# Joined attention blocks: a wait through GpSimd in place of TensorE's drain between the halves of the own products

## The chip, the core and the metric

The kernel runs on one core of a Trainium2 chip. The core has four engines that compute: TensorE (PE; its weight loads are listed apart as PEld), VectorE (DVE), ScalarE (ACT) and GpSimd (POOL). SyncE (SP) issues the DMA transfers. Each engine works through its own queue in order, and engines wait for each other by semaphores. The metric is the time of one execution on the device in microseconds; lower is better.

## What is computed

A linear attention with a decaying state over 768 steps, for 4 batches of 8 heads with 48 features, and then a feed-forward layer with a leaky activation on its output:

```
for t in range(S):
    cur = u * k_t (outer) v_t
    y[:, :, t] = r_t @ (state + cur)
    state = w_t[:, None] * state + k_t (outer) v_t
x = y as [3072 tokens, 384]
h = x @ w_in                       # 384 -> 2048
g = max(h, 0) + alpha * min(h, 0)
out = g @ w_out                    # 2048 -> 384
```

## The kernel before

The attention is cut into 24 blocks, q = 0 to 23: 12 chunks of 64 steps, each for two pairs of batches. A block's loads are wd, kr, rk and nv (decays, keys and queries by feature, queries and keys by step, values). VectorE scales kr by products of decays; GpSimd multiplies rk (L407, two multiplications per block: by u, then by the keys) and VectorE sums it into cd (L410), from which ScalarE makes the diagonal of the block's weights `at` (L415). TensorE makes the scores (L439), which VectorE puts into `at` (L444). The state of each batch pair lives in St and is scaled by GpSimd (L425) and added to by VectorE (L589).

`outputs` emits a block's products on TensorE. All work in it is on quarters of the array, 64 rows by 64 columns. Its parts, in the order in which they are issued from block 8 on:

- `carried` (L509): queries times the old state, 16 products;
- the first half of the own products, `own(True)` (L490, recorded at L482): 8 products, `at` times the values nv, where the row half of the array agrees with the bank (`yb[0]` or `yb[1]`) that the product writes;
- the scores of the next block, `sc` (L435, recorded at L439), 16 products, when the next block is joined to this one;
- the new part of the state, `state` (L516, recorded at L524), 16 products, absent in the last chunk (blocks 22 and 23);
- `other` (L526): a drain of TensorE, and then the second half of the own products, `own(False)`, 8 products that write the same two banks from the other row half.

The two halves write the same banks from different row halves of the array, and the kernel is written so that they do not do this at the same time: the drain keeps them apart. The profile counts two weight loads for each of these products: 16 loads for 8 products, 32 for 16. Blocks 8 to 22 carry the scores of the following block with them: these fifteen are the joined blocks. In blocks 0 to 7 and in block 23 the drain follows the first half directly.

Between the blocks TensorE runs the feed-forward layer: `moe_up` (L677; a bank of nine products, then ScalarE's L683 and VectorE's L685 make pos, ScalarE's L690 and VectorE's L691 split it into gh and gl) and `moe_down` (L705). A check of the inputs runs beside it late in the kernel: SyncE loads raw tiles (L796) and ScalarE works on them (L804 and L813).

A planner written into the kernel sets the order of all engines' work beforehand, from durations that stand in the code. A whole block's products are one operation to it, so what stands inside an operation does not move the others. The order of each queue is then fixed.

Of the kernel before, what the change touches and what calls it, by code (L numbers as in the profile page):

```python
# [33 lines left out]
GT = 3 * P  # L34
ROWS = (slice(0, D), slice(64, R2))
FULL = (slice(0, 64), slice(64, P))
VW = H * 64


# [185 lines left out]
def fast_path(tc, wgt, flag, dmaj, nat, u, ud, vg, wts, alpha, out, part):  # L225
# [4 lines left out]
    nc = tc.nc  # L230
# [7 lines left out]
    with tc.tile_pool(name="const", bufs=1) as const, tc.tile_pool(name="psum", bufs=1, space=PSUM) as psum:  # L238
        def ring(name, shape, n, dtype=F32, pool=const, ordered=True):
            return Ring([pool.tile(shape, dtype, name=f"{name}_{i}") for i in range(n)], ordered)  # L240
# [4 lines left out]
        bank = ring("bank", [P, 512], 5, pool=psum, ordered=False)  # L245
# [24 lines left out]
        r_rk = ring("rk", [P, 2 * HD], 2)  # L270
        r_nv = ring("nv", [P, VW], 3)
        r_suf = ring("suf", [P, SC], 1)
# [12 lines left out]
        extra = Tensor(r_os), Tensor(r_pos)  # L285
# [16 lines left out]
        def c_mask():  # L302
            nc.gpsimd.memset(mask, 1)
            nc.gpsimd.affine_select(out=mask, in_=mask, compare_op=ALU.is_gt, fill=0,
                                    base=0, pattern=[[1, P]], channel_multiplier=-1)
            nc.gpsimd.tensor_copy(out=mask[FULL[1], 0:TK], in_=mask[FULL[1], TK:P])

        def c_ident2():
            for i in range(2):
                nc.gpsimd.tensor_copy(out=ident2[FULL[i]], in_=ident[FULL[i], i * TK:(i + 1) * TK])  # L310
        op("POOL", 0.4, c_ident2, r=["ident"], w=["ident2"])
# [36 lines left out]
        def load(q):  # L348
# [8 lines left out]
            if natural:  # L357
                op("SP", 0.4, lambda: nc.sync.dma_start(out=rk.ap, in_=nat[q, :, 0:2 * HD]), w=[rk], lat=1.1)
            op("SP", 0.4, lambda: nc.sync.dma_start(out=nv.ap, in_=nat[q, :, 2 * HD:2 * HD + VW]), w=[nv], lat=0.75)
            if q < GROUPS[0]:  # L360
# [69 lines left out]
        def scores(q):  # L430

            kr, nv, at = ready[q]
            sps = [Tensor(bank), Tensor(bank)]

            def products():  # L435
                for p in range(NP):
                    for o, i in ORDER:
                        ts = slice(i * TK, (i + 1) * TK)
                        nc.tensor.matmul(sps[o].ap[FULL[i], p * TK:(p + 1) * TK], lhsT=kr.ap[FULL[o], 0, p, ts],  # L439
                                         rhs=kr.ap[FULL[o], 1, p, ts], start=True, stop=True)  # L440

            def rest():
                for o in range(2):
                    op("DVE", 0.46, lambda o=o: nc.vector.copy_predicated(  # L444
                        out=at.ap[:, o], mask=mask[:, 0:TK].unsqueeze(1).broadcast_to([P, NP, TK]), data=pairs(sps[o].ap[:, 0:NP * TK], TK)),
                       r=["mask", sps[o]], w=[(at, o)])
            return products, [(kr, 0), (kr, 1)], sps, rest
# [15 lines left out]
        def outputs(q, nxt):  # L463
# [7 lines left out]
            kr, nv, at = ready.pop(q)  # L471
# [4 lines left out]
            yb = Tensor(r_op if g == 0 else bank), Tensor(bank)  # L476
            up = c < NC - 1
            open_, last = set(), [None]

            def mm(t, rows, cols, stop=False, **kw):  # L480

                last[0] = nc.tensor.matmul(t.ap[rows, cols], start=(t, rows.start) not in open_, stop=stop, skip_group_check=True, **kw)  # L482
                open_.add((t, rows.start))
                return last[0]

            def col(place, i):
                return slice(place % 2 * P + i * TK, place % 2 * P + (i + 1) * TK)


            def own(same):  # L490


                for j in range(2):
                    for o, e in ORDER:
                        i, p = o if same else 1 - o, 2 * j + e
                        h = o * NP + p
                        if g > 0 or 2 * o + j < KT:
                            mm(yb[o], FULL[e], col(j, i), not same, lhsT=nv.ap[FULL[i], h * 64:(h + 1) * 64],
                               rhs=at.ap[FULL[i], o, p, :])
                if g == 0:  # L500


                    for k in range(KT):
                        for e in range(2):
                            i = k // 2 if same else 1 - k // 2
                            mm(yb[k // 2], FULL[e], col(k, i), not same, lhsT=extra[q].ap[FULL[i], (2 * k + e) * 64:(2 * k + e + 1) * 64],
                               rhs=at.ap[FULL[i], 1, 2 + e, :])

            def carried():  # L509
                for j in range(2):  # L510
# [5 lines left out]
            def state(ub, u0, mm):  # L516
                for p in range(NP):
                    for i, o in ORDER:
                        h = o * NP + p
                        mm(ub[i], FULL[o], slice(u0 + p * D, u0 + (p + 1) * D), lhsT=kn[FULL[i], p, FULL[o]],  # L520
                           rhs=nv.ap[FULL[i], h * 64:h * 64 + D])
# [1 line left out]
            def alone(t, rows, cols, **kw):  # L523
                nc.tensor.matmul(t.ap[rows, cols], start=True, stop=True, **kw)  # L524

            def other():  # L526


                nc.tensor.drain()
                own(False)  # L530

            def take(last):

# [23 lines left out]
            if g == 0:  # L557
                def products():
                    own(True)
                    other()  # L560
                op("PE", 1.2, products, r=[(at, 0), (at, 1), nv, extra[q], "ident"], w=yb, kind="QQ", due=due_att[q] + 1.4)
                ub, u0 = (Tensor(bank), Tensor(bank)), 0
                op("PE", 0.5, lambda: state(ub, 0, alone), r=["kn", nv], w=ub, kind="QQ", due=due_att[q] + 10.0)
            else:
                sc, sc_r, sc_w, rest = scores(nxt) if nxt else (None, [], [], None)
                ub, u0 = (sc_w, 256) if nxt else (yb, 256)

                def products():
                    if up and not sc:
                        state(ub, u0, mm)  # L570
                    if c > 0:
                        carried()
                    own(True)
                    if sc:
                        sc()
                        if up:
                            state(ub, u0, alone)
                    other()
                t = 0.8 + (0.47 if c > 0 else 0) + (0.47 if up else 0) + (0.47 if sc else 0)
                op("PE", t, products, r=[(at, 0), (at, 1), nv, "kn", "ident", *([(f"St{m}", i) for i in range(2)] if c > 0 else []), (kr, 1), *sc_r],  # L580
                   w=[*yb, *sc_w], kind="QQ", due=due_att[q] + t)
# [265 lines left out]
def general_path(tc, wgt, dmaj, nat, u, wts, out, xd):  # L847
# [5 lines left out]
    with tc.tile_pool(name="g_st", bufs=1) as st, tc.tile_pool(name="g_wk", bufs=1) as wk, \  # L853
# [12 lines left out]
        for c in range(NC):  # L866
            with tc.For_i(0, TK, 1) as t:
# [10 lines left out]
                for b in range(B):  # L878
                    src = nv[c, b // 2][ds(t + b % 2 * TK, 1), 2 * HD:2 * HD + VW].rearrange("t (o p e) -> o (t p) e", o=2, e=64)[:, :, 0:D]
                    for o in range(2):  # L880
# [113 lines left out]
def layout(r, k, v, w, u, moe_w_in, moe_w_out, moe_alpha):  # L994
# [14 lines left out]
    def natural(a):  # L1009
        return a.reshape(NM, 2, H, NC, TK, D).transpose(3, 0, 1, 4, 2, 5).reshape(NQ, P, HD)  # L1010

    vp = np.zeros((NQ, P, H, 64), v.dtype)
    vp[..., :D] = natural(v).reshape(NQ, P, H, D)
    nat = np.concatenate([natural(r), natural(k), vp.reshape(NQ, P, VW)], axis=2)

# [42 lines left out]
```

## Time and profile before

| what | value |
|---|---|
| time, median of 3 runs | 527.22 us (526.35 to 529.82) |
| span of the profiled execution | 527.3 us |
| TensorE products busy | 506.4 us (96%) |
| TensorE weight loads busy | 475.4 us (90%) |
| VectorE busy | 346.3 us (66%) |
| ScalarE busy | 301.0 us (57%) |
| GpSimd busy | 74.5 us (14%) |

The page gives for the profiled execution its span alone; it stands 0.1 us above the median of the runs. Busy time of the products is not a measure of how well TensorE is used, since products overlap and their ends are modelled; idle times ahead of weight loads say more. In the views, "issue" means that an engine was idle and waited for nothing that the profile shows.

### The profile page before, as it was taken

How to read it: one execution, taken by the hardware profiler on the slowest of the kernel's cores; microseconds unless marked ns; L12 is line 12 of the kernel's file. 1: busy time of each engine (PE TensorE's matmuls, PEld its weight loads, DVE VectorE, ACT ScalarE, POOL GpSimd, SP SyncE). 2: the span in 40 equal slices, each digit the busy share in tenths (PEclk: the TensorE clock that was granted, in tenths of full speed). 3: DMA queues.
4: the chain of work that ended last, by engine and by line, in shares of the span. 5: the costliest groups of instructions: out<-in, count | busy, mean ns of one | idle time of the engine just before them, and what ended most of it. 6: DMA issues, size and time to landing. Idle time of an engine off the chain costs nothing.

```text
span 527.3 us, 13761 instructions
## 1 busy us (share of the span) xinstructions
PE 506.4 (96%) x5654; PEld 475.4 (90%) x5654; DVE 346.3 (66%) x657; ACT 301.0 (57%) x806; POOL 74.5 (14%) x100
## 2 busy tenths in 40 slices
PE   9996999999999999999999999999999999999993
PEld 8974677789999999999999989999999999999992
DVE  6989798999888988868336655577663434434331
ACT  4763754765344566656555556676776666633441
POOL 2011110352001534213000210121000000000000
PEclk9998999999999999999999999999999999999998
DMA  8877678765221668465423556346462035000101
GB/s 301 295 249 261 202 258 277 251 209 153 74 100 49 205 189 265 124 187 154 105 64 107 166 149 211 118 167 189 133 221 89 10 103 197 2 16 10 38 1 37
DMA packets 31945, 78.27 MB, mean 148 GB/s; under 512 B 4480, under 2 KB 13184, under 8 KB 31872
## 3 DMA queue, kind: packets, MB, share of 16 engines
q1 hardware_dynamic: 31872, 77.30, 46.5%
q8 instruction: 46, 0.75, 0.6%
q14 instruction: 27, 0.22, 0.1%
HBM read 66.27 MB, written 6.29 MB: 138 GB/s over the span
## 4 chain that ended last, share of the span: by engine, by line
PE 86%; DMA 6%; DVE 4%; issue 1%; ACT 1%; SPq 0%; DVEq 0%
PE bank L677 37%; PE op L705 33%; PE bank L482 6%; PE op L699 5%; DMA wl<-cx 3%; PE bank L439 2%; DMA raw<-in_wts_dram 2%; PE bank L457 1%; PE bank L524 1%; DMA kr<-in_dmaj_dram 1%; DVE suf L377 1%; PE bank L752 1%; DVE wd L383 0%; DVE cx L652 0%; DVE cx L648 0%
## 5 line engine op out<-in xcount | busy, mean ns | idle before, releaser
L677 PE MATMUL bank<-x,wh 128*128 128x384 f32 (+1 forms) x864 | 230.4, 328 | 0.4 <-ACT cd L403 0.3
L677 PEld LDWEIGHTS bank<-x,wh 128*128 128x128 f32 x864 | 153.5, 188 | 5.4 <-ACT at L415 0.7
L683 ACT ACTIVATE pos<-bank,alpha_n 128x384 f32<-128x384 f32 (+1 forms) x144 | 78.6, 546 | 110.5 <-PE bank L677 110.3
L677 PE MATMUL bank<-x,wl 128*128 128x384 f32 (+1 forms) x432 | 137.2, 318 | 0.0
L685 DVE SCALAR_TENSOR_TENSOR pos<-bank,pos 128x384 f32<-128x384 f32 (+1 forms) x144 | 73.5, 511 | 92.8 <-ACT pos L683 92.6
L705 PE MATMUL op<-wh,gh 128*128 128x384 f32 x336 | 112.9, 336 | 0.7 <-ACT gh L690 0.7
L705 PE MATMUL op<-wh,gl 128*128 128x384 f32 x336 | 112.5, 335 | 0.2 <-DVE gl L691 0.2
L705 PE MATMUL op<-wl,gh 128*128 128x384 f32 x336 | 112.5, 335 | 0.0
L691 DVE TENSOR_TENSOR gl<-pos,gh 128x384 fp32r<-128x384 f32 (+1 forms) x120 | 69.8, 582 | 50.3 <-ACT gh L690 49.3
L677 PEld LDWEIGHTS bank<-x,wl 128*128 128x128 f32 x432 | 81.4, 188 | 2.2 <-DVE wl L622 0.2
L690 ACT CAST gh<-pos 128x384 fp32r<-128x384 f32 (+1 forms) x120 | 58.8, 490 | 36.6 <-DVE pos L685 35.9
L705 PEld LDWEIGHTS op<-wh,gh 128*128 128x128 f32 x336 | 63.2, 188 | 1.5 <-ACT gh L690 1.3
L705 PEld LDWEIGHTS op<-wh,gl 128*128 128x128 f32 x336 | 63.2, 188 | 0.7 <-DVE gl L691 0.7
L705 PEld LDWEIGHTS op<-wl,gh 128*128 128x128 f32 x336 | 63.1, 188 | 0.0
L425 POOL TENSOR_TENSOR St<-St,pc_all 128x192 f32<-128x192 f32 x44 | 27.9, 646 | 221.2 <-DVE St L589 139.1
L415 ACT ACTIVATE at<-ident,cd 128x64 f32<-128x64 f32 x192 | 53.4, 343 | 8.5 <-PE bank L482 7.7
L699 PE MATMUL op<-wl,pos 128*128 128x384 f32 x96 | 37.3, 508 | 6.1 <-DMA wl<-cx 4.9
L407 POOL TENSOR_TENSOR rk<-rk,u_bc 128x384 f32<-128x384 f32 x18 | 21.3, 1185 | 122.5 <-DMA rk<-in_nat_dram 118.4
L377 DVE TENSOR_TENSOR_SCAN suf<-wd,low 128x528 f32<-128x528 f32 x23 | 29.2, 1269 | 4.5 <-DMA wd<-in_dmaj_dram 4.5
L383 DVE TENSOR_TENSOR_SCAN wd<-wd,low 128x528 f32<-128x528 f32 x23 | 29.6, 1288 | 0.1
L699 PEld LDWEIGHTS op<-wl,pos 128*128 128x128 f32 x96 | 16.8, 195 | 14.0 <-DVE kr L389 3.9
L444 DVE COPY_PREDICATED at<-mask,bank 128x256 f32<-128x256 int32 x48 | 19.0, 438 | 10.3 <-PE bank L524 7.9
(107 smaller groups left out, 535.0 us busy)
## 6 DMA issues: line engine op xcount, KB each, us to landing
raw<-in_wts_dram SPq DMA_DIRECT2D x32, 768.0 KB, 5.2
kr<-in_dmaj_dram SPq DMA_DIRECT2D x24, 512.0 KB, 4.4
rk<-in_nat_dram SPq DMA_DIRECT2D x18, 384.0 KB, 3.5
raw<-in_dmaj_dram SPq DMA_DIRECT2D x12, 528.0 KB, 4.2
nv<-in_nat_dram SPq DMA_DIRECT2D x24, 256.0 KB, 4.4
wd<-in_dmaj_dram SPq DMA_DIRECT2D x23, 264.0 KB, 3.4
out_dram<-os SPq DMA_DIRECT2D x46, 96.0 KB, 2.2
wl<-cx SPq DMA_DIRECT2D x13, 192.0 KB, 4.8
```

Of the source, the lines that this page charges most:

```text
L377: op("DVE", 1.28, lambda: nc.vector.tensor_tensor_scan(out=suf.ap[:, ::-1], data0=wv()[:, ::-1], data1=low[:, ::-1], initial=0.0, op0=ALU. ...
L383: op("DVE", 1.28, lambda: nc.vector.tensor_tensor_scan(out=wv(), data0=wv(), data1=low, initial=0.0, op0=ALU.mult, op1=ALU.max), r=["low"] ...
L415: nc.scalar.activation(out=at.ap[:, o, p, :], in_=ident2, func=AF.Copy, scale=cd.ap[:, o * NP + p:o * NP + p + 1])
L425: op("POOL", 0.5, lambda i=i: nc.gpsimd.tensor_tensor(out=St[m][:, i, :, 0:D], in0=St[m][:, i, :, 0:D], in1=pc_all[:, q, i::2].unsqueeze(2 ...
L482: last[0] = nc.tensor.matmul(t.ap[rows, cols], start=(t, rows.start) not in open_, stop=stop, skip_group_check=True, **kw)
L677: nc.tensor.matmul(hp.ap[:, 0:w], lhsT=a[:, j, 0, ks], rhs=x.ap[:, xi, k, 0:w], start=(i == 0), stop=(i == 3 * KT - 1))
L683: op("ACT", us(0.6), lambda: nc.scalar.activation(out=pos.ap[:, 0:w], in_=hp.ap[:, 0:w], func=AF.Relu, scale=alpha_n[:, j:j + 1]), r=[hp, ...
L685: op("DVE", us(0.58), lambda: nc.vector.scalar_tensor_tensor(out=pos.ap[:, 0:w], in0=hp.ap[:, 0:w], scalar=0.0, in1=pos.ap[:, 0:w], op0=AL ...
L690: op("ACT", us(0.54), lambda: nc.scalar.copy(out=gh.ap[:, 0:w], in_=pos.ap[:, 0:w]), r=[pos], w=[gh])
L691: op("DVE", us(0.6), lambda: nc.vector.tensor_tensor(out=gl.ap[:, 0:w], in0=pos.ap[:, 0:w], in1=gh.ap[:, 0:w].bitcast(F32), op=ALU.subtrac ...
L699: nc.tensor.matmul(ops_[s].ap[:, 0:DM], lhsT=gh.ap[:, s * P:(s + 1) * P], rhs=wl[:, j, 1, :].bitcast(F32), start=(j == j0), stop=(j == j1 ...
L705: nc.tensor.matmul(ops_[s].ap[:, 0:DM], lhsT=a.ap[:, ts], rhs=w[:, j, 1, :], start=(j == j0 and i == 0), stop=(j == j1 - 1 and i == 2))
```

## The change

`other` no longer drains TensorE in a joined block. Behind the first half, `passing` puts a no-operation into GpSimd's queue that depends on the last product emitted so far (the last of the first half); the first product of the second half depends on that no-operation. Blocks that are not joined keep the drain.

```
+SYNC = mybir.DependencyInfo(mybir.DependencyClass.Sync, mybir.DependencyReason.DATA)
             def own(same):
+                made = []
...
-                            mm(yb[o], FULL[e], col(j, i), not same, lhsT=nv.ap[FULL[i], h * 64:(h + 1) * 64],
-                               rhs=at.ap[FULL[i], o, p, :])
+                            made.append(mm(yb[o], FULL[e], col(j, i), not same, lhsT=nv.ap[FULL[i], h * 64:(h + 1) * 64],
+                                           rhs=at.ap[FULL[i], o, p, :]))
...
+                return made[0]
...
-            def other():
-                nc.tensor.drain()
-                own(False)
+            def passing():
+                sign = nc.gpsimd.nop()
+                tc.add_manual_dep(sign.ins, last[0].ins.name, SYNC, reason="row groups of a bank")
+                return sign
+
+            def other(passed=None):
+                if passed is None:
+                    nc.tensor.drain()
+                    own(False)
+                    return
+                tc.add_manual_dep(own(False).ins, passed.ins.name, SYNC, reason="row groups of a bank")
...
                     own(True)
+                    passed = passing() if sc else None
                     if sc:
                         sc()
                         if up:
                             state(ub, u0, alone)
-                    other()
+                    other(passed)
```

The order of TensorE's products is the same as before. In block 8 the end of the state, the second half and the first product of the feed-forward layer stand so on TensorE before (the drain, which these rows do not list, stands between the second and the third row; names of banks carry their number):

```order
L524 MATMUL bank_79<-nv_110,kn 64x48
L524 MATMUL bank_78<-nv_110,kn 64x48
L482 MATMUL bank_76<-at_114,nv_110 64x64
L482 MATMUL bank_77<-at_114,nv_110 64x64
L482 MATMUL bank_76<-at_114,nv_110 64x64
```

and now, with the semaphore that a row waits for in brackets:

```order
L527 MATMUL bank_79<-nv_110,kn 64x48
L527 MATMUL bank_78<-nv_110,kn 64x48
L483 MATMUL bank_76<-at_114,nv_110 64x64 [waits Pool_sequencer_49]
L483 MATMUL bank_77<-at_114,nv_110 64x64
L483 MATMUL bank_76<-at_114,nv_110 64x64
```

Nothing moved but that the third row now waits for GpSimd. On GpSimd's queue, at block 9 (the scaling of St, and the multiplications of rk for blocks 12 and 13), before:

```order
L425 TENSOR_TENSOR St_93<-St_93,pc_all 128x4x48 [waits DVE_49,PE_49,Activation_49]
L425 TENSOR_TENSOR St_93<-St_93,pc_all 128x4x48 [waits DVE_49,PE_49]
L407 TENSOR_TENSOR rk_106<-rk_106 128x384 [waits Pool_49]
L407 TENSOR_TENSOR rk_107<-rk_107,u_bc 128x384 [waits DMAHW2_49]
L407 TENSOR_TENSOR rk_107<-rk_107 128x384 [waits Pool_49]
```

and now:

```order
L426 TENSOR_TENSOR St_93<-St_93,pc_all 128x4x48 [waits DVE_49,PE_49,Activation_49]
L426 TENSOR_TENSOR St_93<-St_93,pc_all 128x4x48 [waits DVE_49,PE_49]
L408 TENSOR_TENSOR rk_106<-rk_106 128x384 [waits PE_49,Pool_49]
L408 TENSOR_TENSOR rk_107<-rk_107,u_bc 128x384 [waits DMAHW2_49]
L408 TENSOR_TENSOR rk_107<-rk_107 128x384 [waits Pool_49]
```

The no-operation itself is not listed; the wait for TensorE that it brings is printed with the next instruction, so it stands here between the second and the third row. At block 13 (rk for block 18), before:

```order
L425 TENSOR_TENSOR St_93<-St_93,pc_all 128x4x48 [waits DVE_49,PE_49]
L407 TENSOR_TENSOR rk_106<-rk_106,u_bc 128x384 [waits DMAHW4_49,DVE_49]
L407 TENSOR_TENSOR rk_106<-rk_106 128x384 [waits Pool_49]
L425 TENSOR_TENSOR St_94<-St_94,pc_all 128x4x48 [waits DVE_49,PE_49,Activation_49]
L425 TENSOR_TENSOR St_94<-St_94,pc_all 128x4x48 [waits DVE_49,PE_49]
```

and now:

```order
L426 TENSOR_TENSOR St_93<-St_93,pc_all 128x4x48 [waits DVE_49,PE_49]
L408 TENSOR_TENSOR rk_106<-rk_106,u_bc 128x384 [waits DMAHW4_49,DVE_49]
L408 TENSOR_TENSOR rk_106<-rk_106 128x384 [waits PE_49,Pool_49]
L426 TENSOR_TENSOR St_94<-St_94,pc_all 128x4x48 [waits DVE_49,PE_49,Activation_49]
L426 TENSOR_TENSOR St_94<-St_94,pc_all 128x4x48 [waits DVE_49,PE_49]
```

Here the no-operation stands between the two multiplications of rk, behind one that waits for a transfer.

## Rows read from the trace of the kernel before

**Rows 1.** The page's head, and the shares of its chain by engine.

```profile
span 527.3 us, 13761 instructions
...
PE 86%; DMA 6%; DVE 4%; issue 1%; ACT 1%; SPq 0%; DVEq 0%
```

**Rows 2.** The drain's line: count, ns at least/median/most, first and last start.

```profile
L529 PEldq DRAIN  x24: 468/520/637, 14.9 to 458.0; - x24
```

**Rows 3.** Timeline at block 8: start us, us, engine line op, operands, count [idle before].

```profile
167.59 0.33 PEld L482 LDWEIGHTS bank<-at,nv 64*64 64x64 f32 x16
...
167.65 0.41 PE L482 MATMUL bank<-at,nv 64*64 64x64 f32 x16
...
167.83 0.56 PEld L439 LDWEIGHTS bank<-kr 64*64 64x64 f32 x32
...
168.29 0.56 PEld L524 LDWEIGHTS bank<-nv,kn 64*64 64x64 f32 x32
...
169.14 0.33 PEld L482 LDWEIGHTS bank<-at,nv 64*64 64x64 f32 x16 [0.28 <-issue]
```

**Rows 4.** Groups of weight loads, 160 to 520 us: count | busy, mean ns | idle before.

```profile
L482 PEld LDWEIGHTS bank<-at,nv 64*64 64x64 f32 x512 | 10.6, 134 | 4.4 <-issue 4.4
L482 PEld LDWEIGHTS bank<-kr,St 64*64 64x64 f32 x512 | 8.9, 134 | 4.0 <-issue 4.0
```

**Rows 5.** Timeline of weight loads: block 9's second half, block 22 and the next load.

```profile
179.44 0.33 PEld L482 LDWEIGHTS bank<-at,nv 64*64 64x64 f32 x16 [0.23 <-issue]
...
440.43 0.56 PEld L439 LDWEIGHTS bank<-kr 64*64 64x64 f32 x32
441.29 0.33 PEld L482 LDWEIGHTS bank<-at,nv 64*64 64x64 f32 x16 [0.29 <-issue]
441.69 0.19 PEld L677 LDWEIGHTS bank<-x,wh 128*128 128x128 f32 x1
```

**Rows 6.** Timeline: TensorE waits for GpSimd, and GpSimd for VectorE.

```profile
0.81 0.20 POOL L289 MEMSET os<- 128x128 f32 x1 [0.29 <-POOLq L1045]
...
1.07 0.50 PEld L744 LDWEIGHTS bank<-os 128*128 128x128 f32 x2 [1.07 <-POOL os L289]
...
223.46 0.35 DVE L589 TENSOR_TENSOR St<-bank,St 128x192 f32<-128x192 f32 x1
...
223.98 0.51 POOL L425 TENSOR_TENSOR St<-St,pc_all 128x192 f32<-128x192 f32 x1 [5.35 <-DVE St L589]
```

**Rows 7.** GpSimd's waits at line 425: count, ns at least/median/most.

```profile
L425 POOLq EVENT_SEMAPHORE  x37: 17/17/43, 50.9 to 419.6; - x37
```

**Rows 8.** Timeline at block 13: the rk transfer's issue, GpSimd and the scores' loads.

```profile
230.77 0.67 SPq L358 DMA_DIRECT2D rk<-in_nat_dram  x1
...
236.12 1.02 POOL L407 TENSOR_TENSOR rk<-rk,u_bc 128x384 f32<-128x384 f32 x1 [10.55 <-DMA rk<-in_nat_dram]
...
237.14 0.56 PEld L439 LDWEIGHTS bank<-kr 64*64 64x64 f32 x32
```

**Rows 9.** Timeline: GpSimd and VectorE behind block 9, and VectorE at block 22.

```profile
175.04 1.46 POOL L407 TENSOR_TENSOR rk<-rk 128x384 f32<-128x384 f32 x1
...
185.63 0.53 DVE L410 TENSOR_REDUCE cd<-rk 128x8 f32<-128x384 f32 x1
...
439.99 0.56 DVE L685 SCALAR_TENSOR_TENSOR pos<-bank,pos 128x384 f32<-128x384 f32 x1 [0.99 <-ACT pos L683]
```

**Rows 10.** Waits of weight loads, 160 to 520 us: total us, times, longest.

```profile
PEld op L705 <- ACT gh L690: 1.3, 2, 1.1
```

**Rows 11.** Timeline behind block 15: two transfers' issues, ScalarE, and TensorE's load.

```profile
298.16 0.33 SPq L359 DMA_DIRECT2D nv<-in_nat_dram  x1
298.58 0.38 SPq L796 DMA_DIRECT2D raw<-in_wts_dram  x1
...
307.42 0.54 ACT L813 ACTIVATE raw<-raw 128x384 f32<-128x384 f32 x1 [3.30 <-DMA raw<-in_wts_dram]
...
308.41 0.19 PEld L705 LDWEIGHTS op<-wh,gh 128*128 128x128 f32 x1 [1.06 <-ACT gh L690]
```

More of the change, by code (lines that the diff above doesn't have):

```diff
@@ L505, in own @@
                             i = k // 2 if same else 1 - k // 2
-                            mm(yb[k // 2], FULL[e], col(k, i), not same, lhsT=extra[q].ap[FULL[i], (2 * k + e) * 64:(2 * k + e + 1) * 64],
-                               rhs=at.ap[FULL[i], 1, 2 + e, :])
+                            made.append(mm(yb[k // 2], FULL[e], col(k, i), not same, lhsT=extra[q].ap[FULL[i], (2 * k + e) * 64:(2 * k + e + 1) * 64],
+                                           rhs=at.ap[FULL[i], 1, 2 + e, :]))
+                return made[0]
             def carried():
```

## The prediction

> **What bounds the kernel now.** Read the page first: of the chain of work that ended last, 86% lies on TensorE, 6% on transfers, 4% on VectorE, in a span of 527.3 us [rows 1]. So time taken out of TensorE's queue counts, as long as nothing else becomes late. Next, the drain's own line: 24 drains between 14.9 and 458.0 us, 0.52 us each in the middle [rows 2]. A drain's duration is not its price, since older loads and products still run under it. The price is read from the weight loads around it.
>
> The joined blocks lie between 167 and 442 us. In the first of them (q8) the loads are four runs and a hole [rows 3]: first half of the own products from 167.59 (16 loads), scores from 167.83 (32), state from 168.29 (32), second half from 169.14 with 0.28 us of idle ahead of it. A run starts before the loads of the run ahead have ended: from scores to state it is 168.29 − 167.83 = 0.46 us for 32 loads, though the run itself lasts 0.56. At this pace the second half would start at 168.29 + 0.46 = 168.75. It starts at 169.14, so the drain costs **0.38 us**: 0.28 of idle and the 0.10 by which runs otherwise overlap.
>
> **The change part by part.** Fifteen blocks (q8 to q22) lose the drain; the other nine keep it.
>
> *Removed.* From 160 us on, the loads of the own products have 4.4 us of "issue" idle ahead of them [rows 4]. These are the drains of q8 to q23, sixteen of them, of which fifteen go: 4.4 × 15/16 = 4.1 us. To it comes the overlap, 15 × 0.10 = 1.5. Sum: **5.6 us**. The other way: 15 × 0.38 = 5.7, of which q9 with 0.23 of idle in place of 0.28 [rows 5] takes 0.05. Same answer. In q22 there is no state run, and the second half would start at 440.43 + 0.46 = 440.89 and not at 441.29 [rows 5], 0.40 earlier.
>
> *Added.* A no-operation in GpSimd's queue waits for the last product of the first half; TensorE's first product of the second half waits for it. In q8 the first half's products end at 167.65 + 0.41 = 168.06 [rows 3], and the second half is due at 168.75: a window of **0.69 us**, filled by scores and state. The way there and back has three pieces. GpSimd to TensorE: a memset ends at 0.81 + 0.20 = 1.01, the loads that wait for it start at 1.07, so 0.06 us [rows 6]. The instruction itself: waits in GpSimd's queue last 17 ns, at most 43 [rows 7]. TensorE to GpSimd is not shown alone. Bounds: nothing at the least; at the most what GpSimd takes to start a computation behind VectorE, 223.46 + 0.35 = 223.81 to 223.98, 0.17 us [rows 6]. So there and back takes 0.02 + 0.06 = 0.08 us at the least and 0.17 + 0.04 + 0.06 = 0.27 at the most. I take 0.2, near the upper end, since a product's end in the profile is modelled and its signal may come later. Both ends lie well inside 0.69, so in fourteen blocks the wait costs nothing, hidden by scores and state. Without that cover it would cost 0.2 each, 3 us in all. In q22 the cover is the scores alone: the first half ends 0.23 after the scores' loads begin (168.06 − 167.83), at 440.66, and 0.23 us remain until 440.89. There the wait costs 0 to 0.04. The sum stays 5.6.
>
> The last product of each first half now also signals by itself. No row shows that price apart. At the least it is nothing, at the most the product would hold TensorE for the 0.06 us of the hop above, 0.9 us in fifteen blocks; I take nothing, since the runs of loads follow each other at one pace in q8 though products inside them signal to other engines.
> The Trainium skill (TensorE: Matmul & The Clock Gate, "The cost: per-tile semaphore tail") says that such increments are handled one after the other and gives about 26 ns for each. By that page 15 × 26 ns = 0.4 us would come back, an estimate that makes the time 522.1; no run here shows it.
>
> *What stands ahead of the no-operation on GpSimd.* If GpSimd is still at work or waiting when the first half ends, TensorE stands too. By the order and GpSimd's rows the tightest block is q13; in the others the instruction ahead has ended microseconds before. In q13 it is the first multiplication into rk, which begins at 236.12 when its transfer has landed, and ends at 236.12 + 1.02 = 237.14 [rows 8]. The scores' loads begin at 237.14, so the first half ends 0.23 later, at 237.37, and the second half is due 2 × 0.46 later, at 238.06. The no-operation is free 0.23 us before it is wanted, and 0.9 before TensorE would feel it. The transfer was issued at 230.77, behind a reduction of VectorE in a queue that follows TensorE's banks, so it moves with TensorE.
>
> *What stands behind it.* GpSimd may no longer run ahead of TensorE. In q9 the second multiplication into rk began at 175.04; now it waits for the end of the first half, which is 1.08 us before the second half's loads (169.14 − 168.06 in q8), at 179.44 − 1.08 = 178.36 [rows 5, 9]: 3.3 us late. It takes 1.46 and ends at 179.8; VectorE's reduction of it starts at 185.63 [rows 9], which leaves 5.8 us. In q12, q15 and q18 multiplications are held in the same way, by 4 us and less, and their reductions come later still. Cost: nothing.
>
> *What is late next.* Each step behind a join comes up to 0.4 us earlier on TensorE. Behind q22 the next load (441.69) needs a bank that VectorE's pos gave free at 439.99 + 0.56 = 440.55 [rows 5, 9], 1.1 us ahead; 0.7 would be left. From 160 us on, the loads waited for ScalarE twice, 1.3 us in all, 1.1 of it once [rows 10]: at 308.41 a gh stood behind a check of the weights whose transfer, issued at 298.58, was there at 307.42, 8.8 us later [rows 11]. The issue stands right behind that of nv at 298.16, which must wait for q15's second half; so both move with TensorE and this wait stays as it is.
>
> **The sum.** 527.3 − 5.6 = **521.7 us**. The profiled execution's span is 527.3 and the median of the runs 527.22, so nothing is added for what lies around it. Against the median this is −1.05%, on the edge of the 1% that a measurement of this kernel can tell from no change.
>
> **The rivals.**
> 1. *Given back at 308.* If the check's transfer lands at a fixed time and not 8.8 us behind its issue, TensorE waits longer there by what the eight joins before it (q8 to q15) won, 8 × 0.37 = 3.0 us: 524.7. For: ScalarE stood 3.30 us on this transfer [rows 11]. Against: its issue follows TensorE. Chance 0.12.
> 2. *The emptying stays.* The change would not do what it says if TensorE emptied itself here without a drain. For: the carried products, which open each 64-row stretch, have 4.0 us of "issue" idle ahead of them with no drain there [rows 4]. Against: inside the block first half, scores and state follow each other with no idle [rows 3], in the same 64×64 form as the second half. Then all 5.6 us stay: 527.3. Chance 0.08.
> The Trainium skill (TensorEngine Tiling (Array Packing), "Key Properties") says that a change of tiling mode drains TensorE and a change of tile alone does not; the trace agrees, with idle at the entries and none from run to run.
> 3. *Slower: TensorE behind a transfer.* In q13 GpSimd reaches the no-operation only after the rk transfer and 1.02 us of multiplication. Where it lands L later than now, TensorE stands for L − 0.9. It took 236.12 − 230.77 = 5.3 us [rows 8]. At 8.8 us, the worst above, L is 3.5, the loss 2.6 and the time 524.3. To be slower than before it must take 5.3 + 0.9 + 5.6 = 11.8 us; with 13.5 the loss is 7.3 and the time 529.0. Nothing in the rows takes so long. Chance 0.05.
> 4. *More than forecast.* If the check's transfer at 298.58 takes 7.7 us and not 8.8, the 1.1 us at 308 are gone too: 520.6. Chance 0.07.
>
> **How the numbers follow.** The forecast, all fifteen holes closed and nothing given back, has chance 0.68, and its own range is 521.0 to 522.8 (up to 0.9 worse for the signals; runs of one kernel went from 526.35 to 529.82). The range 520.5 to 524.8 takes in rivals 1 and 4 and leaves out rival 2 and most of 3, with some of each case's edges: about 0.82. Faster by over 1% means below 521.95: 0.41 of the forecast's 0.68 and rival 4, together 0.48. Slower by over 1% is rival 3's far end: 0.04. Within 1%: 0.48.
>
> **What would show it.** The loads of the second half should start 0.46 us after the state run starts, without idle, in fourteen blocks, and 0.46 after the scores in q22; the "issue" idle of the own products from 160 us on should fall from 4.4 to about 0.3. It is wrong if those loads show an idle that GpSimd's queue releases, if the load at 308 waits about 4 us in place of 1.1, or if an rk reduction holds VectorE.

## The result: 520.7 us, 1.3% faster

Run side by side, the changed kernel takes 520.7 us (median of 4 runs, 520.26 to 521.01) and the kernel before 527.98 (median of 4, 526.35 to 529.82): ratio 0.987, 95% interval 0.984 to 0.990. A second comparison, on another occasion, gave 522.33 against 527.18: ratio 0.989, interval 0.985 to 0.993 (the two medians alone would make 0.991, which lies inside it). The forecast was 521.7. It was right in its direction, its mechanism and its range, though not in every step, as the last part shows. But 7.3 us between the first two medians are more than the 5.6 that the sum had, and the experiments below were made to find where the rest is from.

The page of the changed kernel, its head and the shares of its chain (before: [rows 1]):

```profile
span 519.2 us, 13761 instructions
...
PE 85%; DMA 8%; DVE 3%; SPq 1%; ACT 1%; issue 1%; POOL 0%; DVEq 0%; POOLq 0%
```

TensorE still carries the chain. The weight loads of block 8 answer to [rows 3] (timeline: start us, us, engine line op, operands, count, [idle before]; the lines of the file have moved: 482 is now 483, 439 is 440, 524 is 527, 705 is 719):

```profile
165.68 0.33 PEld L483 LDWEIGHTS bank<-at,nv 64*64 64x64 f32 x16
165.91 0.56 PEld L440 LDWEIGHTS bank<-kr 64*64 64x64 f32 x32
166.38 0.56 PEld L527 LDWEIGHTS bank<-nv,kn 64*64 64x64 f32 x32
166.85 0.33 PEld L483 LDWEIGHTS bank<-at,nv 64*64 64x64 f32 x16
167.24 0.19 PEld L719 LDWEIGHTS op<-wh,gh 128*128 128x128 f32 x1
```

The second half starts 166.85 − 166.38 = 0.47 us behind the start of the state run, with no idle; it was 0.85 before. The groups of loads from 160 to 520 us (as [rows 4]) and the no-operation's line (as [rows 7]):

```profile
L483 PEld LDWEIGHTS bank<-at,nv 64*64 64x64 f32 x512 | 10.6, 135 | 0.2 <-issue 0.2
L483 PEld LDWEIGHTS bank<-kr,St 64*64 64x64 f32 x512 | 8.9, 134 | 4.0 <-issue 4.0
```

```profile
L532 POOLq EVENT_SEMAPHORE  x15: 17/17/17, 166.2 to 432.8; - x15
```

The idle ahead of the own products fell from 4.4 us to 0.2 (the last drain, in block 23), that of the carried products stayed at 4.0. TensorE never waits for the no-operation, in fifteen blocks.

**Where the 8.1 us between the two profiles went.** I follow the start of each block's carried products through both timelines; a step is the time from one such start to the next. The two spans differ by 527.3 − 519.2 = 8.1:

| piece | changed minus before, us |
|---|---|
| block 8's carried products start (165.22 against 167.13) | −1.9 |
| fifteen joins, block 8 to block 22 | −6.0 |
| TensorE's wait at 308 (now at 302) | −0.9 |
| a new wait of 0.4 at 422 | +0.4 |
| from block 23 to the end | +0.3 |

Only the second row is at the places of the edit. The first row stands ahead of all of them.

### The profile page after: what moved, and what is told of

It reads as the page before. It is cut to its first block, busy times and chain, and to the rows that moved or that the text cites. A ratio compares the mean times of both kernels' runs of the same rounds, so it can differ in the third digit from the quotient of the medians.

```text
span 519.2 us, 13761 instructions
## 1 busy us (share of the span) xinstructions
PE 501.7 (97%) x5654; PEld 473.4 (91%) x5654; DVE 345.6 (67%) x657; ACT 300.3 (58%) x806; POOL 74.4 (14%) x100
## 4 chain that ended last, share of the span: by engine, by line
PE 85%; DMA 8%; DVE 3%; SPq 1%; ACT 1%; issue 1%; POOL 0%; DVEq 0%; POOLq 0%
PE bank L691 36%; PE op L719 32%; PE bank L483 5%; PE op L713 5%; DMA raw<-in_wts_dram 4%; DMA wl<-cx 3%; PE bank L440 2%; PE bank L458 1%; PE bank L527 1%; PE bank L758 1%; SPq L614 1%; PE bank L766 1%; PE bank L401 1%; DVE cx L662 0%; DVE cx L666 0%
## 5 line engine op out<-in xcount | busy, mean ns | idle before, releaser
L705 DVE TENSOR_TENSOR gl<-pos,gh 128x384 fp32r<-128x384 f32 (+1 forms) x120 | 68.0, 567 | 51.2 <-ACT gh L704 50.6
L713 PE MATMUL op<-wl,pos 128*128 128x384 f32 x96 | 35.9, 492 | 5.7 <-DMA wl<-cx 4.2
L378 DVE TENSOR_TENSOR_SCAN suf<-wd,low 128x528 f32<-128x528 f32 x23 | 30.4, 1321 | 4.3 <-DMA wd<-in_dmaj_dram 4.3
```

What stands on the lines that cost most here:

```text
L378: op("DVE", 1.28, lambda: nc.vector.tensor_tensor_scan(out=suf.ap[:, ::-1], data0=wv()[:, ::-1], data1=low[:, ::-1], initial=0.0, op0=ALU. ...
L705: op("DVE", us(0.6), lambda: nc.vector.tensor_tensor(out=gl.ap[:, 0:w], in0=pos.ap[:, 0:w], in1=gh.ap[:, 0:w].bitcast(F32), op=ALU.subtrac ...
L713: nc.tensor.matmul(ops_[s].ap[:, 0:DM], lhsT=gh.ap[:, s * P:(s + 1) * P], rhs=wl[:, j, 1, :].bitcast(F32), start=(j == j0), stop=(j == j1 ...
```

## The experiments

### A second profile of each kernel

> The kernel before once more, for a second profile of it. Theory 1 (the early 1.9 us are no part of the change): the carried products of block 8, the first joined one, start 0.5 to 2.5 us earlier or later than in the first profile of before although nothing is changed, and the two profiles differ by up to 3 us in the load-bound stage between 20 and 63 us. Theory 2 (the change reaches the early stage too): both profiles of before agree there within 0.3 us. The wait of 1.1 us at 308 (weight load behind ScalarE's gh, behind the check transfer): theory 1 expects it again only if that transfer takes 8 us or more again.

> The changed kernel once more, timed closely. Theory 1 (the join gives 15 x 0.40 = 6.0 us, and what the first pair of medians shows beyond it, 1.3 us, is the spread of before's runs): ratio 0.988 to 0.990. Theory 2 (the change also wins at 308 and in the early stage): 0.984 to 0.987. The steps from block to block between block 8 and block 22 repeat within 0.1 us.

| profile of | block 8 starts at | blocks 8 to 23 | span | run's time |
|---|---|---|---|---|
| before, first | 167.13 | 290.36 | 527.3 | not given |
| before, second | 167.52 | 288.90 | 525.8 | 527.55 |
| changed, first | 165.22 | 283.91 | 519.2 | 520.97 |
| changed, second | 169.61 | 282.91 | 522.2 | 523.95 |

The carried products of blocks 8 and 23 in the second profiles, of before and of the changed kernel:

```profile
167.52 0.56 PEld L482 LDWEIGHTS bank<-kr,St 64*64 64x64 f32 x32 [0.25 <-issue]
...
456.42 0.56 PEld L482 LDWEIGHTS bank<-kr,St 64*64 64x64 f32 x32 [0.25 <-issue]
```

```profile
169.61 0.56 PEld L483 LDWEIGHTS bank<-kr,St 64*64 64x64 f32 x32 [0.25 <-issue]
...
452.52 0.56 PEld L483 LDWEIGHTS bank<-kr,St 64*64 64x64 f32 x32 [0.25 <-issue]
```

The start of block 8 moves by 4.4 us between two executions of the one changed kernel, and over the thirteen profiles of kernels that are alike up to there it lies anywhere from 164.6 to 170.4, with the drains or without. The two profiles of before differ there by only 0.4 (0.5 to 2.5 were expected), so that pair alone would not have shown the spread. With the changed kernel's pair, the first row of the table of pieces turns out to be the spread of executions and not the change. It arises in the stretch that waits for transfers. A row each of the changed kernel, first and second profile (20 to 64 us: busy time of each engine, granted clock, share of the DMA engines, GB/s):

```profile
20.00:64.00 44.00, 38.07 (x497) 31.03 (x496) 38.65 (x66) 28.36 (x80) 5.26 (x6) 1.00 0.74 248
```

```profile
20.00:64.00 44.00, 38.38 (x475) 30.67 (x476) 37.43 (x62) 26.04 (x76) 4.54 (x6) 0.88 0.65 217
...
44.00:52.00 8.00, 6.31 (x16) 4.23 (x17) 5.47 (x10) 3.37 (x6) 0.00 (x0) 0.50 0.68 246
```

The same work: in the first the granted clock is 1.00 all through, in the second it is 0.50 from 44 to 52 us, the lower of its two levels, 1.2 GHz, behind a hole of 3.54 us in which TensorE waited (the row below), and the profile counts 22 products fewer between 20 and 64 us.

```profile
44.64 0.50 PEld L713 LDWEIGHTS op<-wl,pos 128*128 128x128 f32 x2 [3.54 <-DVE wl L636]
```

The start of block 8 goes with the mean granted clock of this stretch, 20 to 64 us, in all thirteen profiles, with some overlap in the middle: at 1.00 it lies at 164.6 and 165.2 (two profiles), at 0.96 from 166.1 to 167.5 (four, both of before among them), at 0.92 at 166.9 and 168.3 (two), at 0.88 from 168.4 to 170.4 (five). The first profile of the changed kernel is one of the two without any lower clock there, and its 1.9 us are no merit of the change.

Between blocks 8 and 23 the two second profiles, which have no wait at 308, compare cleanly: 282.91 − 288.90 = **−5.99 us for fifteen joins, 0.40 each** (from 0.35 to 0.42, block by block). With 527.2 this makes a ratio of 0.9886, which is inside both intervals.

### The wait at 308

No kernel of its own was needed for this: each profile is one more case. ScalarE's first step on the check's weights and TensorE's loads behind it, in the first profile of the changed kernel and below it in the second profile of before (before, first: [rows 11]):

```profile
301.50 0.54 ACT L827 ACTIVATE raw<-raw 128x384 f32<-128x384 f32 x1 [2.44 <-DMA raw<-in_wts_dram]
...
302.49 0.19 PEld L719 LDWEIGHTS op<-wh,gh 128*128 128x128 f32 x1 [0.22 <-ACT gh L704]
303.08 0.19 PEld L719 LDWEIGHTS op<-wh,gl 128*128 128x128 f32 x1 [0.41 <-DVE gl L705]
```

```profile
304.88 0.56 ACT L813 ACTIVATE raw<-raw 128x384 f32<-128x384 f32 x1 [0.39 <-DMA raw<-in_wts_dram]
```

| profile | ScalarE stood | TensorE stood for gh |
|---|---|---|
| before, first | 3.30 | 1.06 |
| no-operation on SyncE | 3.08 | 0.85 |
| signal behind the cover | 2.88 | 0.66 |
| three writes on GpSimd | 2.55 | 0.33 |
| changed, first | 2.44 | 0.22 |
| changed, second | 1.29 | 0 |
| before, second | 0.39 | 0 |

TensorE's wait is what ScalarE's exceeds 2.2 us by, in every row to within 0.04 us. Of the six other profiles only the one with the drain put back has a wait for gh (0.21, where ScalarE stood 2.43). So the place is as the prediction read it (a gh behind the check), but the wait belongs neither to the kernel nor to the change: kernels with the change show from 0 to 0.85 us, kernels with the emptying in place 0 to 1.06. Once it is there, 0.40 to 0.41 more follow for gl. The wait at 422 is of the same kind (0 in both profiles of before and in the second of the changed kernel, 0.41 in its first). Five of the thirteen profiles show it, and none of the four that drain in the joined blocks, so whether the change makes it likelier stays open.

### The drain put back beside the no-operation

```
 def other(passed=None):
     ...
+    nc.tensor.drain()
     tc.add_manual_dep(own(False).ins, passed.ins.name, SYNC, ...)
```

> The changed kernel with the drain put back: in the fifteen joined blocks the no-operation on GpSimd stays, TensorE waits for it, and it empties itself as well. Theory 1 (the drain is the whole price, holding GpSimd costs and gains nothing): all of the gain goes back, 0.998 to 1.001 against before, and the 'issue' idle ahead of the own products is 4 us and more again. Theory 2 (part of the gain comes from GpSimd's later start, by which transfers and VectorE lie otherwise): part of it stays, 0.990 to 0.996. If holding GpSimd costs, slower than before: above 1.002.

Ratio 1.000 (0.998 to 1.003). The idle ahead of the own products is 4.4 us again:

```profile
L483 PEld LDWEIGHTS bank<-at,nv 64*64 64x64 f32 x512 | 10.6, 134 | 4.4 <-issue 4.4
```

Each step from block to block is that of the first profile of before to within 0.04 us, with the one exception of block 15 to 16, where the wait at 308 was shorter. So all of the gain is the drain's, and holding GpSimd back neither costs nor gains. This was theory 1.

### A second drain in each joined block

```
                     own(True)
                     if sc:
+                        nc.tensor.drain()
                         sc()
```

> The kernel before with a second drain in each joined block, between the first half of the own products and the scores. Theory 1 (a drain costs 0.38 to 0.40 us wherever it stands between two runs of 64x64 products, since TensorE must empty and fill again): 15 x 0.40 = 6.0 us more than before in the blocks 8 to 22, 1.010 to 1.013. Rival (the price depends on what runs ahead: 16 loads in place of 32 leave less to empty): under 0.2 us each, 1.000 to 1.006.

In this one the kernel before has two drains in each of the fifteen blocks. Ratio 1.011 (1.004 to 1.018). Blocks 8 to 23 take 294.69 us, 5.79 more than the second profile of before, 0.39 for each added drain. Its block 8:

```profile
168.87 0.33 PEld L482 LDWEIGHTS bank<-at,nv 64*64 64x64 f32 x16
169.44 0.56 PEld L439 LDWEIGHTS bank<-kr 64*64 64x64 f32 x32 [0.24 <-issue]
169.90 0.57 PEld L524 LDWEIGHTS bank<-nv,kn 64*64 64x64 f32 x32
170.75 0.33 PEld L482 LDWEIGHTS bank<-at,nv 64*64 64x64 f32 x16 [0.28 <-issue]
```

Scores start 169.44 − 168.87 = 0.57 us behind the first half, where 0.23 was usual: 0.34 at the place itself. The whole step of block 8 grew by 0.32, the fifteen steps by 0.30 to 0.47. So with 16 loads ahead the price is on average that with 32 ahead (0.39 and 0.40).

### The signal given behind the cover

The cover is the work that TensorE has between the signal and its use: the scores and the state run.

```
 def alone(t, rows, cols, **kw):
-    nc.tensor.matmul(t.ap[rows, cols], start=True, stop=True, **kw)
+    last[0] = nc.tensor.matmul(t.ap[rows, cols], start=True, stop=True, **kw)
 ...
-                    passed = passing() if sc else None
                     if sc:
                         sc()
                         if up:
                             state(ub, u0, alone)
-                    other(passed)
+                    other(passing() if sc else None)
```

> The no-operation waits for the last product of the state run (in block 22 for that of the first half, as in the changed kernel) in place of the last product of the first half: the same way there and back, without scores and state as its cover. Theory 1 (the cover hides a round trip of 0.08 to 0.27 us behind the products' ends): TensorE stands in fourteen blocks as long as a drain takes and for the round trip on top of it, 14 x (0.4 + 0.08 to 0.27) = 6.7 to 9.4 us more than the changed kernel: 1.001 to 1.006 against before. Rival (a wait does not let TensorE run as empty as a drain does, the drain costs more than the emptying alone): between 0.990 and 0.998. Rival (the round trip is long, 0.5 us and more): above 1.010.

Ratio 1.000 (0.997 to 1.003): the whole gain is gone, and no more than that. Block 8 and the group of own products:

```profile
171.52 0.56 PEld L527 LDWEIGHTS bank<-nv,kn 64*64 64x64 f32 x32
172.37 0.32 PEld L483 LDWEIGHTS bank<-at,nv 64*64 64x64 f32 x16 [0.29 <-POOLq L532]
...
L483 PEld LDWEIGHTS bank<-at,nv 64*64 64x64 f32 x512 | 10.5, 134 | 4.2 <-POOLq L532 4.0 <-issue 0.2
```

From the state run to the second half 172.37 − 171.52 = 0.85 us, exactly what the drain took [rows 3]. I had expected the drain's price and the round trip on top of it; the two cost the same. A wait without cover is as dear as a drain: **what brought the gain is the distance between the signal and its use**, not the exchange of one instruction for another. In block 22 the signal stayed where it was, and its second half shows no wait.

### How wide the window is

```
 def passing():
-    sign = nc.gpsimd.nop()
-    tc.add_manual_dep(sign.ins, last[0].ins.name, SYNC, ...)
+    for _ in range(3):                  # 5 in the other kernel
+        sign = nc.gpsimd.memset(pad, 0.0)
+        tc.add_manual_dep(sign.ins, last[0].ins.name, SYNC, ...)
     return sign
```

> In place of the no-operation GpSimd carries out three writes of zeros into a scratch tile of 128x128 (0.20 us each by the row of the same form) between the first half and the second: 0.61 us of work in the window that the prediction put at 0.69. Theory 1 (window 0.69, way there and back 0.08 to 0.27 us): TensorE stands 0 to 0.2 us in each of fourteen joined blocks, 0 to 2.7 us in all, so 0.988 to 0.994 against before, and the idle ahead of the own products is 0.2 to 3 us. Rival (the window is hardly there: the first half ends only when the second is due): TensorE stands 0.5 us and more each, 7 us and more, 1.001 or above. Other rival (there is much more room than 0.69): idle as in the changed kernel, 0.2 us.

> The same with five writes, 1.02 us, more than the window. Theory 1: 1.02 + 0.08 to 0.27 - 0.69 = 0.4 to 0.6 us of waiting for GpSimd in each of fourteen blocks, 0.2 more in block 22, 6 to 9 us in all over the changed kernel: 1.000 to 1.006 against before. From three to five writes the idle ahead of the own products grows by 14 x 0.41 = 5.7 us at the most. Other rival (much more room): 0.988 to 0.992, as the changed kernel.

Ratios 0.995 (0.992 to 0.998) and 1.012 (1.004 to 1.020). Block 8 with five writes (TensorE's products and loads, GpSimd), and the group of own products with five:

```profile
166.60 0.41 PE L484 MATMUL bank<-at,nv 64*64 64x64 f32 x16
...
167.11 1.25 POOL L534 MEMSET pad<- 128x128 f32 x5 [5.42 <-PE bank L484]
...
168.41 0.33 PEld L484 LDWEIGHTS bank<-at,nv 64*64 64x64 f32 x16 [0.60 <-POOL pad L534]
...
L484 PEld LDWEIGHTS bank<-at,nv 64*64 64x64 f32 x512 | 10.5, 134 | 10.2 <-POOL pad L534 10.0 <-issue 0.2
```

Here both hops can be read: the first half ends at 166.60 + 0.41 = 167.01 and GpSimd starts at 167.11, 0.10 us later; it ends at 168.36 and the load starts at 168.41, 0.05 later. There and back is **0.15 us** in this block without the instruction itself. Five writes last 1.25 and not 1.02, since each waits for the one ahead, 0.06 between them; that is what my expectation lacked, and why this kernel is slower than I said. With the window of 0.69 the second half should come 1.25 + 0.15 − 0.69 = 0.71 us late. It was due 0.47 behind the state run's start (167.25), at 167.72, and came at 168.41: 0.69 late. With three writes (0.73 us) it should be 0.73 + 0.15 − 0.69 = 0.19; the second half comes 172.08 − 171.44 = 0.64 behind the state run, 0.17 late. Block 8 and the group of own products there:

```profile
171.30 0.73 POOL L534 MEMSET pad<- 128x128 f32 x3 [5.42 <-PE bank L484]
...
171.44 0.56 PEld L528 LDWEIGHTS bank<-nv,kn 64*64 64x64 f32 x32
172.08 0.32 PEld L484 LDWEIGHTS bank<-at,nv 64*64 64x64 f32 x16
...
L484 PEld LDWEIGHTS bank<-at,nv 64*64 64x64 f32 x512 | 10.5, 134 | 2.6 <-POOL pad L534 0.9 <-issue 0.2
```

The hops are read from the same rows, so what these sums check is the window. Over the fourteen blocks with a state run the second half is 0.17 to 0.24 us late with three writes and 0.69 to 0.76 with five, so the window of 0.69 holds within 0.05, and the no-operation uses about 0.17 of it. Block 22, with the scores alone as cover, does not fit as well: there the second half is 1.01 us late with three writes, where 0.73 + 0.15 − 0.23 = 0.65 was due, since GpSimd started 0.46 us behind the first half's end in place of 0.10. Why it did is open.

### The wait in another queue

```
-    sign = nc.gpsimd.nop()
+    sign = nc.vector.nop()        # or nc.scalar.nop(), or nc.sync.nop()
```

> The no-operation stands in VectorE's queue in place of GpSimd's. In most joined blocks the instruction right behind it is a gl, whose product on TensorE has ended before the block begins and which now has to wait for the first half, and the products right behind the block need gl. Theory 1 (the wait is free only on an engine with nothing due behind it): part of the gain goes, or all of it: 0.992 to 1.010 against before, with TensorE waiting for gl (VectorE) behind the joined blocks where it did not. Rival (any engine will do): 0.987 to 0.990, as the changed kernel, and no wait for gl of over 0.5 us in all.

> The no-operation stands in ScalarE's queue, behind evictions and copies that follow TensorE closely. Theory 1: in some blocks ScalarE is late by more than 0.57 us, the room that three and five writes on GpSimd showed (0.73 us of work made TensorE stand 0.16), and TensorE stands there; blocks 8 to 22 take 1 us and more longer than in the changed kernel (288.9 before, 282.9 changed, from block 8's start to block 23's). Rival (any queue will do): within 0.6 us of 282.9.

> The no-operation stands in SyncE's queue, which issues the transfers; transfers behind it can be issued only when the first half has ended, and the no-operation itself can be late behind an issue that waits for VectorE or for a transfer. Theory 1 (the place is free only where the queue runs neither late nor far ahead): two things can cost, transfers that start up to some microseconds later, and TensorE waiting where SyncE is late; 0.990 to 1.010 against before, with waits of TensorE's second halves for SyncE's queue. Rival (any queue will do): 0.987 to 0.990 and no such wait.

VectorE: 0.989 (0.983 to 0.996). SyncE: 0.989 (0.985 to 0.994). ScalarE, one run: 521.95 us. All three are as fast as the changed kernel within what the runs can tell, and no second half waits for the no-operation in any of them. My theory fell in all three, at the size that it gave. From block 8 to 23 they take 283.66 (VectorE), 284.31 (SyncE) and 283.64 us (ScalarE), and the changed kernel 282.91 and 283.91. Of the 0.73 us that ScalarE's kernel takes longer than the second profile of the changed one (a little more than the rival gave), 0.76 are the wait of the kind of that at 422; of SyncE's 1.40, 1.26 are the wait at 308, at which the check's transfer came late. Whether the no-operation had a part in that transfer's lateness is open; kernels without it show the same. One loss is VectorE's own, in block 11 (its timeline, and TensorE's):

```profile
202.79 0.21 DVE L381 RECIPROCAL low<-suf 128x8 f32<-128x8 f32 x1 [2.85 <-PE bank L483]
203.03 1.26 DVE L384 TENSOR_TENSOR_SCAN wd<-wd,low 128x528 f32<-128x528 f32 x1
204.20 0.53 DVE L699 SCALAR_TENSOR_TENSOR pos<-bank,pos 128x384 f32<-128x384 f32 x1
```

```profile
204.79 0.19 PEld L691 LDWEIGHTS bank<-x,wh 128*128 128x128 f32 x1 [0.61 <-DVE pos L699]
```

VectorE stood 2.85 us on the no-operation, then had 1.5 us of work that it could have done in that time, and TensorE waited 0.61 for the pos behind it. Behind block 22 it waited 0.23 more for a pos. In the other thirteen blocks there was room.

### What a signal costs

```
+    for m in first[1:15:2]:             # products of the first half
+        tc.add_manual_dep(nc.gpsimd.nop().ins, m.ins.name, SYNC, ...)
     sign = nc.gpsimd.nop()
```

> The changed kernel with three more products of each first half signalling by themselves (45 signals in all), and one more no-operation in GpSimd's queue that waits for them. Prediction's term (a signal costs nothing): the steps from block to block stay within 0.03 us of the changed kernel's. The rule of the Trainium skill, about 26 ns for each signal (TensorE: Matmul & The Clock Gate, 'The cost: per-tile semaphore tail'): each step grows by 3 x 0.026 = 0.08 us, 1.2 us over fifteen blocks. The prediction's upper end (0.06 us each): 0.18 us a step, 2.7 us.

From block 8 to block 14 each step is the same as in the changed kernel to 0.01 us (−0.40, −0.36, −0.40, −0.41, −0.40, −0.42 against the second profile of before). Three more signals in a block cost nothing that can be seen; 0.08 a block would be.

The Trainium skill (TensorE: Matmul & The Clock Gate, "The cost: per-tile semaphore tail") counts about 26 ns for each increment, which are handled one after the other. These runs don't show it. Other products run for 0.7 us behind the signals here, and whether that is what hides them was not tried.

### Six more drains taken out

```
-                ub, u0 = (sc_w, 256) if nxt else (yb, 256)
+                cover = up and not nxt
+                ub, u0 = (sc_w, 256) if nxt else ((Tensor(bank), Tensor(bank)) if cover else yb, 256)
 ...
-                    if up and not sc:
-                        state(ub, u0, mm)
 ...
-                    passed = passing() if sc else None
+                    passed = passing() if sc or cover else None
                     if sc:
                         sc()
-                        if up:
-                            state(ub, u0, alone)
+                    if up:
+                        state(ub, u0, alone)
```

> The changed kernel, and in the six blocks 2 to 7, which have no scores of the next block to cover the wait, the state run goes to two banks of its own and is moved between the halves as cover for a no-operation in place of the drain. Theory 1 (0.4 us for each drain that lies on the path; blocks 2 and 3 lie in the stretch that waits for transfers): 4 x 0.4 = 1.6 us less than the changed kernel, 0.984 to 0.988 against before. Rival (the early blocks wait for transfers, or two more banks hold up other work there): no faster than the changed kernel, 0.988 to 0.995.

Ratio 1.013 (1.007 to 1.019), slower than before and outside both expectations. The six drains are gone, but the op now takes two more banks, and the planner set another order for everything behind it. TensorE's largest wait in this kernel, and the busy time up to 167 us here and, below, in the second profile of the changed kernel:

```profile
PE bank L401 <- DVE rk L374: 5.0, 1, 5.0
...
0.00:167.00 167.00, 153.02 (x1825) 132.19 (x1826) 139.37 (x247) 90.77 (x252) 31.47 (x50) 0.96 0.65 212
```

```profile
0.00:167.00 167.00, 158.29 (x1840) 135.93 (x1841) 141.65 (x249) 92.98 (x258) 31.12 (x48) 0.97 0.63 208
```

Up to 167 us TensorE has been busy 5.3 us less; and over the whole span its products take 510.1 us in place of 505.0, with 40 more of them. These two make 10.4 of the 10.9 us by which the spans differ. Which part of the new order does it, the banks or the places, was not tried. No kernel of this study beats the changed one.

## Why the prediction was right, point by point

- **The price of a drain** (0.38 us, the sum of 5.6). Right in its mechanism and short by 0.4 us in its size. At block 8 the join itself gives 0.38, as worked out from [rows 3]; within the ten weight loads behind the block the lead grows to 0.40, in block 9 from 0.33 to 0.36. Read over the whole step from block to block, fifteen joins give 5.99. A block of this form without a drain, on which that could have been read, is not in the profile of before. Rival 2, that TensorE empties itself here anyway, fell with the idle ahead of the own products, 4.4 to 0.2 us.
- **The added wait costs nothing.** Right. The way there and back was taken as 0.2 us between 0.08 and 0.27; two hops measured in block 8 make 0.10 + 0.05 and the instruction 0.02. The window of 0.69 held within 0.05 us with three writes and with five. In block 22, where the cover is the scores alone, the second half starts 432.93 − 432.46 = 0.47 behind the scores, so the 0.04 allowed for there is not seen.
- **The signal's price.** Nothing, as taken; 45 signals more didn't show it either.
- **What stands behind the no-operation.** Right. GpSimd's row of the second multiplications shows the hold: 9.3 us in four blocks.

```profile
POOL rk L408 <- PE bank L483: 9.3, 4, 4.4
...
176.31 1.23 POOL L408 TENSOR_TENSOR rk<-rk 128x384 f32<-128x384 f32 x1 [1.65 <-PE bank L483]
...
184.34 0.54 DVE L411 TENSOR_REDUCE cd<-rk 128x8 f32<-128x384 f32 x1
```

  Behind block 9 it ends at 177.54 and VectorE's reduction of it starts at 184.34, 6.8 us later (5.8 were expected). In block 13 the multiplication ahead of the no-operation ended at 231.92 + 1.01 = 232.93, before the scores' loads begin at 233.28. Rival 3 did not come.
- **The wait at 308 stays.** Wrong as a step: one execution's wait was carried over as if it were the kernel's. It is what a transfer's lateness leaves above 2.2 us and was between 0 and 1.06 us in the profiles. Rival 4 named this place and this direction; that the change brings it can't be said, since the second profile of before has no wait there either. Rival 1 asked for 4 us there; no profile shows over 1.06.
- **What lies around the span.** Wrong. "Nothing is added" was concluded from a span of 527.3 and a median of 527.22, which are of different executions. The runs with both numbers have 520.97 − 519.2 = 1.8 and 527.55 − 525.8 = 1.7 us around the span. So the execution that was profiled took about 529, near the slowest of the three runs, and a proper sum from its span would have been 529 − 6.0 for one so slow. The forecast still came within 1.0 us of the median by luck: the 1.8 us left out and that execution's wait at 308 (1.06 + 0.40 for gh and gl) nearly cancel. It should have been made from the median, 527.2 − 5.6 = 521.6, with the 3.5 us between the fastest and the slowest of the three runs in its range.
- **The chance at the edge of 1%.** The gain by the joins, 1.14% of 527.2, lies just beyond it, as the 0.48 to 0.48 said. The interval of the first comparison lies nearly all beyond 1% (1.0 to 1.6), that of the second reaches from 0.7 to 1.5. The first four runs of the changed kernel lay near its fast end (520.3 to 521.0 us) with a mean granted clock of 0.993 to 0.996; the six later ones had 0.986 to 0.992 and took 521.2 to 525.1. That agrees with the early stretch, where the start of block 8 goes with the clock. What gave those four the higher clock stays open.

## What to carry to other kernels

Read the price of a drain from the starts of the runs on both sides of it, not from its own duration: here 0.34 to 0.38 us at the place itself and 0.39 to 0.40 over a whole step, at both places where it was tried. It can be had back where independent work stands between the point that must be passed and the point that needs it: let some queue signal at the first and wait at the second, with more than the there and back (0.15 us here) of other work in between; with no such work, the wait through GpSimd cost as much as the drain. And set a sum against the median of the runs, and a stage's step against a second profile, before a wait that stands once in one profile is taken for the kernel's.

## What I had not expected

- A wait through GpSimd without cover takes TensorE as long as a drain, 0.85 us from the state run's start in both. I had taken the round trip to come on top.
- The queue for the wait could be any: GpSimd's, VectorE's, ScalarE's and SyncE's all give 282.9 to 284.3 us from block 8 to 23, against 288.9. Two of the 45 waits in the three other queues show a loss (0.61 and 0.23 us, both on VectorE). That SyncE's held transfers cost nothing is a measurement of this kernel, where they are issued microseconds ahead.
- The first 165 us of one and the same program vary by 4 us from execution to execution, with a mean granted clock from 0.88 to 1.00 between 20 and 64 us, with which the start of block 8 goes; behind block 8 the steps repeat to 0.03 us apart from the waits at 308 and 422, and small edits can be told apart there from one profile each, which the total time can't do.
